# Deferred gate statistics, GpSimd additions in the last chunk, and an unpadded V, in an adaLN + attention + gMLP kernel

## The chip, the core and the metric

The kernel runs on one core of a Trainium2 chip. The metric is the device time of one execution in microseconds (us); lower is better. Three runs of the kernel before the change took 1346.54, 1346.97 and 1347.03 us; their median is 1346.97 us.

## What is computed

One conditioned transformer block on a sequence of 2048 rows of width 512, cut from the reference to what matters here:

```
sa, ca, ga, sb, cb, gb = split(silu(c) @ w_mod, 6)
h = layernorm(x) * (1 + ca) + sa
q = h @ wq                                   # 32 heads of 128; 8 cached K/V heads of 2048 rows
o = softmax(q @ k.T / sqrt(128)) @ v
x = x + ga * (o @ wo)
h = layernorm(x) * (1 + cb) + sb             # "LN2"
z = gelu(h @ w_in)                           # 2048 x 1792
z1, z2 = z[:, :896], layernorm(z[:, 896:])   # z2 is the gate
g = w_sp @ z2 + b_sp[:, None]                # mixes the 2048 rows
y = x + gb * ((z1 * g) @ w_out)
```

Tensors are bfloat16 in memory; sums are kept in float32.

## The kernel before

The 2048 rows are 16 tiles of 128 rows, four tiles to a chunk of 512. Engines are called by their names or by the abbreviations of the profile: TensorE (PE, and PEld for its weight loads), VectorE (DVE), ScalarE (ACT), GpSimd (POOL) and SyncE (SP, which issues most transfers). Each engine works its instructions off in the order in which the program emits them, and that order is written out by hand: `at(it, slot, fn)` hangs a function on a slot of an iteration, and one loop runs through the iterations and their eight slots.

**Attention.** Iteration `it` below NU = 128 is one K/V head and one row tile. In each of its eight slots it multiplies K by q for four query heads (`qk`, L879), exponentiates on ScalarE (L886) and multiplies the previous iteration's probabilities by V (`pv`, L901). V rows have 128 values and a column of ones behind them, so that the matmul also yields the sum of the probabilities; a row thus has 129 columns that are used. The rows lie DV = 136 elements apart in the tile `v1` (L711, printed as `v`), and the two heads of one PSUM bank `o_ps` lie as far apart (L898). L712 fills the columns from 128 on with ones, and L713 loads the values. L912 and L913 normalise by the sum; SP transposes the result (L921).

**Output projection and LN2.** Three iterations later `wo_proj` multiplies by wo (L933); VectorE adds the result to the tile's accumulator (L946), and for the last K/V head also multiplies by ga (L951), adds x (L952) and takes the tile's statistics for LN2 (L690, L691). `ln2` then hangs three steps on later slots: POOL computes the reciprocal deviation (L671, L675), VectorE normalises (L679, `xn`) and SP transposes (L970), VectorE scales and shifts into hT (L977).

**The MLP's first half, inside iterations 128 to 133.** There `zrun(3)` takes three functions at a time off the list `zq`. It holds first the gate tiles 0 to 11 (`z2_tile`): eight matmuls into a two-bank PSUM buffer s_ps (L1064), a Gelu on ScalarE into `z2` (L1074, printed as `z`), then on VectorE two statistics instructions and their aggregation (L1081, L1082). After each fourth tile follows `z2_norm` of that chunk: POOL computes four reciprocal deviations (L671, L675), and VectorE normalises four tiles in place (L679). Then come the seven z1 tiles of the sequence's first half (`z1_tile`, L1100, Gelu L1108). s_ps has two buffers in all.

After iteration 130 the pool `late` is closed (it holds `pT`, `v1`, `wo_g`, `onorm`, `oT` and the accumulators `xacc`), and the pool `mlp` is opened in its place, with z1T, the weights w_out and b_sp (loaded by POOL's queue, L1160 and L1161), and later two blocks of w_sp. What is written into `mlp` must wait until the last use of `late` is through. After the loop SP is given 32 transposing loads of w_sp (L1012), the rest of `zq` is run, then gate tiles 12 to 15, their normalisation, and the other half of z1.

**The MLP's second half.** For each chunk t of output rows, `spatial` accumulates 16 matmuls over the normalised gate tiles (L1205), and VectorE adds b_sp (L1214, `gb`) and multiplies by z1 (L1215, `yT`). `o2_mm` multiplies by w_out (L1220), and `finish_tile` multiplies by gb (L1235, `tmp`) and adds x (L1236, `yout`), both on VectorE, and stores (L1237). `tmp` and `yout` have two buffers each. The last chunk is done in two parts, of 384 and of 128 columns; in the second part the first three output tiles are finished between the spatial matmuls of f = 1 to 3, and the fourth, in two halves, at the very end.

Of the kernel before, what the change touches and what calls it, by code (L numbers as in the profile page):

```python
# [11 lines left out]
FP32 = mybir.dt.float32  # L12
ACT = mybir.ActivationFunctionType
ALU = mybir.AluOpType
AX = mybir.AxisListType
P = 128
# [4 lines left out]
def _f_chunk(f: int) -> int:  # L21
    for cand in range(512, 0, -1):
        if f % cand == 0:
            return cand
    return 1
# [550 lines left out]
def kernel(  # L576
# [19 lines left out]
    nc = tc.nc  # L596
    _, S, D = A_x.shape
    _, HKV, SK, DH = A_k_cache.shape
# [11 lines left out]
    CT = 512 // P  # L610
    FC = _f_chunk(FH)
    NFHC = FH // FC
    NSLOT = NKT // 2
    DV = DH + 8
    inv_sqrt_dh = 1.0 / math.sqrt(DH)

    NB = HKV * NCH
# [1 line left out]
    out_dram = out[0].rearrange("(t p) d -> p t d", p=P)  # L619
# [18 lines left out]
    stat = fast.enter_context(tc.tile_pool(name="stat", bufs=2))  # L638
# [6 lines left out]
    x_sb = res.tile([P, NT, D], BF16, name="x_sb")  # L645
# [6 lines left out]
    mvz = res.tile([P, NT, nc.vector.BN_AGGR_DIM], FP32, name="mvz")  # L652
# [9 lines left out]
    def bank(name):  # L662
        return psum.tile([P, 512], FP32, name=name)

    def bank2():
        return psum.tile([P, 1024], FP32, name="s_ps")

    def rstd_of(mv, n, tag):

        ve = stat.tile([P, CT], FP32, name=f"ve_{tag}")  # L670
        nc.gpsimd.tensor_scalar(  # L671
            out=ve[:, :n], in0=mv[:, :, 1], scalar1=LN_EPS, scalar2=None, op0=ALU.add
        )
        rstd = stat.tile([P, CT], FP32, name=f"rstd_{tag}")
        nc.gpsimd.tensor_tensor(out=rstd[:, :n], in0=ve[:, :n], in1=mhalf[:, :n], op=ALU.pow)  # L675
        return rstd

    def normalise(dst, src, mv, rstd):
        nc.vector.tensor_scalar(  # L679
            out=dst,  # L680
            in0=src,
            scalar1=mv,
            scalar2=rstd,
            op0=ALU.subtract,
            op1=ALU.mult,
        )
# [23 lines left out]
    def load_v(g, rows, engine):  # L710
        v1 = late.tile([P, NKT, DV], BF16, name="v1")  # L711
        nc.gpsimd.memset(v1[:, :, DH:DV], 1.0)  # L712
        engine.dma_start(out=v1[:, :, 0:DH], in_=rows[:, g])  # L713
        groups[g]["v1"] = v1
# [109 lines left out]
    for hf in range(2):  # L824
        nc.scalar.copy(
            out=kT0[:, hf * SK // 2 : (hf + 1) * SK // 2],
            in_=k_ps[:, hf * SK // 2 : (hf + 1) * SK // 2],
# [36 lines left out]
    NU = HKV * NT  # L864
# [3 lines left out]
    def at(it, slot, fn):  # L868
        later.setdefault((it, slot), []).append(fn)
# [23 lines left out]
    def pv(u, i):  # L893
# [3 lines left out]
        if i % (2 * per) == 0:  # L897
            o_pss[u] = bank("o_ps")[:, 0 : 2 * DV].rearrange("p (h d) -> p h d", h=2)  # L898
        o_ps = o_pss[u]
# [156 lines left out]
    zs = {}  # L1056

    def z2_tile(j):
        ps = {}

        def mm(hf, dt):
            if hf == 0 and dt == 0:
                ps[0] = bank2()
            nc.tensor.matmul(  # L1064
                ps[0][:, hf * 512 : hf * 512 + FC],
                lhsT=h2Ts[j // CT][:, dt, (j % CT) * P : (j % CT + 1) * P],
                rhs=win_sb[:, dt, FH + hf * FC : FH + (hf + 1) * FC],
                start=(dt == 0),
                stop=(dt == NDT - 1),
            )  # L1070
            if hf < NFHC - 1 or dt < NDT - 1:
                return
            z2 = zs["z2"]
            nc.scalar.activation(  # L1074
                out=z2[:, j, :].rearrange("p (h c) -> p h c", h=NFHC),
                in_=ps[0][:].rearrange("p (h c) -> p h c", h=2)[:, 0:NFHC, 0:FC],
                func=ACT.Gelu_apprx_tanh,
            )
            stz = stat.tile([P, NFHC, nc.vector.BN_STATS_DIM], FP32, name="stz")
            for h in range(NFHC):  # L1080
                nc.vector.bn_stats(out=stz[:, h, :], in_=z2[:, j, h * FC : (h + 1) * FC])  # L1081
            nc.vector.bn_aggr(out=mvz[:, j, :], in_=stz[:])  # L1082

        return [lambda hf=hf, dt=dt: mm(hf, dt) for hf in range(NFHC) for dt in range(NDT)]

    def z2_norm(ch):
        rstd = rstd_of(mvz[:, ch * CT : (ch + 1) * CT, :], CT, "lnz")
        for j in range(ch * CT, (ch + 1) * CT):
            z2 = zs["z2"]
            normalise(  # L1090
                z2[:, j, :], z2[:, j, :], mvz[:, j, 0:1], rstd[:, j % CT : j % CT + 1]
            )

    def z1_tile(f, ch2):
        ps = {}

        def mm(k, dt):
            if k == 0 and dt == 0:
                ps[0] = bank2()
            nc.tensor.matmul(  # L1100
                ps[0][:, k * 512 : (k + 1) * 512],
                lhsT=win_sb[:, dt, f * P : (f + 1) * P],
                rhs=h2Ts[2 * ch2 + k][:, dt, :],
                start=(dt == 0),
                stop=(dt == NDT - 1),
            )
            if k == 1 and dt == NDT - 1:
                nc.scalar.activation(  # L1108
                    out=zs["z1T"][:, f, ch2 * 1024 : (ch2 + 1) * 1024],
                    in_=ps[0][:],  # L1110
                    func=ACT.Gelu_apprx_tanh,
                )

        return [lambda k=k, dt=dt: mm(k, dt) for k in range(2) for dt in range(NDT)]

    zq = []
    for j in range(3 * CT):
        zq += z2_tile(j)
        if j % CT == CT - 1:
            zq[-1] = [zq[-1], lambda ch=j // CT: z2_norm(ch)]  # L1120
    for f in range(NFT):
        zq += z1_tile(f, 0)
    zq = [z if isinstance(z, list) else [z] for z in zq]

    def zrun(n):
        for _ in range(min(n, len(zq))):
            for fn in zq.pop(0):
                fn()

    for it in range(NU + 6):  # L1130
        if it < NU:
# [31 lines left out]
    for t in range(1, 3):  # L1163
        wsp[t] = mlp.tile([P, NT, 512], BF16, name=f"wsp{t}")
        for st in range(NT):
            load_wsp(wsp[t], t, st)
    zrun(len(zq))
    for j in range(3 * CT, NT):
        for fn in z2_tile(j):
            fn()  # L1170
    z2_norm(3)
    for f in range(NFT):
        for fn in z1_tile(f, 1):
# [5 lines left out]
        out=ok1[:], in0=rall[:], scalar1=1.0 / SAFE, scalar2=None, op0=ALU.is_ge  # L1179
# [8 lines left out]
        out=bad[:], in0=okm[:], scalar1=-1.0, scalar2=1.0, op0=ALU.mult, op1=ALU.add  # L1188
# [10 lines left out]
    z2, z1T = zs["z2"], zs["z1T"]  # L1199

    def spatial(t, yT, f, c0, n):

        g_ps = bank("misc")
        for st in range(NT):
            nc.tensor.matmul(  # L1205
                g_ps[:, :n],
                lhsT=z2[:, st, f * P : (f + 1) * P],
                rhs=wsp[t][:, st, c0 : c0 + n],
                start=(st == 0),
                stop=(st == NT - 1),  # L1210
            )
        cols = slice(t * 512 + c0, t * 512 + c0 + n)
        gb = mlp.tile([P, 512], BF16, name="gb", bufs=2)
        nc.vector.tensor_tensor(out=gb[:, :n], in0=g_ps[:, :n], in1=bsp_bc[:, cols], op=ALU.add)  # L1214
        nc.vector.tensor_tensor(  # L1215
            out=yT[:, f, c0 : c0 + n], in0=gb[:, :n], in1=z1T[:, f, cols], op=ALU.mult
        )

    def o2_mm(dst, yT, jj, f):
        nc.tensor.matmul(  # L1220
            dst,
            lhsT=yT[:, f, jj * P : (jj + 1) * P],
            rhs=wout_sb[:, f, :],
            start=(f == 0),
            stop=(f == NFT - 1),
        )

    def finish_tile(t, jj, src, parts=1):
        j = t * CT + jj
        tmp = mlp.tile([P, D], FP32, name="tmp", bufs=2)  # L1230
        yout = mlp.tile([P, D], BF16, name="yout", bufs=2)
        w = D // parts
        for k in range(parts):
            s = slice(k * w, (k + 1) * w)
            nc.vector.tensor_tensor(out=tmp[:, s], in0=src[:, s], in1=gb_rows[:, s], op=ALU.mult)  # L1235
            nc.vector.tensor_tensor(out=yout[:, s], in0=tmp[:, s], in1=x_sb[:, j, s], op=ALU.add)  # L1236
            (nc.sync if k == 0 else nc.scalar).dma_start(out=out_dram[:, j, s], in_=yout[:, s])  # L1237

    yTs = {}

# [6 lines left out]
    last = NCH - 1  # L1247
# [16 lines left out]
    o2_last = [acc[jj // 2][:, (jj % 2) * 512 : (jj % 2 + 1) * 512] for jj in range(CT)]  # L1264
# [8 lines left out]
    for f in range(NFT):  # L1273
        spatial(last, yT, f, n_a, P)
        if f == 0:
            for jj in range(CT - 1):
                o2_mm(o2_last[jj], yT, jj, NFT - 1)
        else:
            o2_mm(o2_last[CT - 1], yT, CT - 1, f - 1)
        if 1 <= f < CT:  # L1280
            finish_tile(last, f - 1, o2_last[f - 1])
    o2_mm(o2_last[CT - 1], yT, CT - 1, NFT - 1)
    finish_tile(last, CT - 1, o2_last[CT - 1], parts=2)
    fast.close()

    redo = nc.values_load(flag[0:1, 0:1], min_val=0, max_val=P)
# [35 lines left out]
```

## Time and profile before

| | before |
|---|---|
| median of three runs | 1346.97 us |
| the profiled execution | 1347.03 us |
| its span | 1345.2 us (1.83 us lie around it) |
| TensorE busy (PE) | 1303.1 us, 97% |
| weight loads (PEld) | 860.4 us, 64% |
| ScalarE busy (ACT) | 1079.2 us, 80% |
| VectorE busy (DVE) | 476.3 us, 35% |
| GpSimd busy (POOL) | 46.4 us, 3% |
| the chain that ended last | PE 92%, DVE 3%, SP's queue 2%, issue 1%, DMA 1% |

The chain is followed back from the last instruction to what released each step. By lines it is L879 35%, L901 34%, L843 7%, L933 6%, L1205 6%. The page also cuts the span into 40 slices of 33.6 us and gives each engine's busy share in a slice as one digit of tenths; `PEclk` is the clock that TensorE was granted, in tenths of full speed. A line of a timeline has the start, the duration, the engine, the line of the program, the operation, what it writes and reads, its shape and count, and in square brackets the idle time ahead of it and what ended it. A matmul's printed duration contains its pipeline's latency, so the rate of several is read from their starts. A row of a group has the count, then busy time and mean duration of one in ns, then the idle time before.

### The profile page before, as it was taken

The numbers are of one execution on the slowest core, as the hardware profiler recorded it, in microseconds if no ns is written. First come the engines' busy times: TensorE is split into PE (matmuls) and PEld (weight loads), VectorE is DVE, ScalarE is ACT, GpSimd is POOL, SyncE is SP. The second block draws the span as 40 slices with busy tenths as digits, with TensorE's granted clock in tenths as the row PEclk, the third lists the DMA queues.
The fourth block names the chain that finished last, engine by engine and source line by source line (L and its number), as shares of the span: only waits on it lengthen the run. The fifth ranks groups of instructions, "written<-read, shape, count | busy, mean of one in ns | idle before, by whom it ended". The sixth has DMA issues, their size and how long they took to land.

```text
span 1345.2 us, 27642 instructions
## 1 busy us (share of the span) xinstructions
PE 1303.1 (97%) x12137; PEld 860.4 (64%) x12345; DVE 476.3 (35%) x1171; ACT 1079.2 (80%) x1059; POOL 46.4 (3%) x88
## 2 busy tenths in 40 slices
PE   6999999999999999999999999999999999979997
PEld 4666666666666666666666666666666666534444
DVE  5442222222222222222222222222222666873344
ACT  4789999999999999999999999999999999540000
POOL 1010000000000000000000000000000000110000
PEclk9999999999999999999999999999999999989999
DMA  8120021102211120012010410121111111143200
GB/s 274 29 64 17 13 63 37 21 17 35 62 20 21 32 68 17 17 37 68 17 20 13 84 21 17 21 64 32 21 20 17 29 29 33 25 110 83 67 20 26
DMA packets 141184, 56.53 MB, mean 42 GB/s; under 512 B 131105, under 2 KB 136353, under 8 KB 141057
## 3 DMA queue, kind: packets, MB, share of 16 engines
q1 hardware_dynamic: 137504, 42.17, 15.0%
q0 software_dynamic: 3408, 12.45, 3.5%
q8 instruction: 98, 1.61, 0.5%
q14 instruction: 30, 0.24, 0.1%
q10 hardware_dynamic: 144, 0.07, 0.0%
HBM read 21.63 MB, written 2.10 MB: 18 GB/s over the span
## 4 chain that ended last, share of the span: by engine, by line
PE 92%; DVE 3%; SPq 2%; issue 1%; DMA 1%; POOL 0%; ACT 0%; ACTq 0%; POOLq 0%; DVEq 0%
PE s_ps L879 35%; PE o_ps L901 34%; PE misc L843 7%; PE misc L933 6%; PE misc L1205 6%; PE s_ps L1100 2%; SPq L1012 1%; PE o_ps L1220 1%; PE s_ps L1064 1%; DMA wq_g<-in_A_wq_dram 1%; DVE stz L1081 1%; DVE hT L803 0%; PE s_ps L1220 0%; PE misc L796 0%; DVE bnst L690 0%
## 5 line engine op out<-in xcount | busy, mean ns | idle before, releaser
L886 ACT ACTIVATE pT<-s_ps 128x1024 bf16<-128x1024 f32 x1024 | 1045.6, 1024 | 92.2 <-PE s_ps L879 16.5
L901 PEld LDWEIGHTS <-pT 128*128 128x128 bf16 x8192 | 548.5, 98 | 241.2
L901 PE MATMUL o_ps<-v,pT 128*128 128x129 bf16 x8192 | 631.4, 220 | 0.0
L879 PE MATMUL s_ps<-qT,kT 128*128 128x512 bf16 x2048 | 609.9, 379 | 10.8 <-DVE qT L852 0.8
L912 DVE RECIPROCAL rall<-o_ps 128x2 f32<-128x2 f32 x256 | 43.6, 170 | 750.9 <-PE o_ps L901 750.7
L879 PEld LDWEIGHTS <-kT 128*128 128x128 bf16 x2048 | 199.8, 98 | 120.1 <-issue 1.3
L843 PE MATMUL misc<-hT,wq_g 128*128 128x512 bf16 (+2 forms) x462 | 169.1, 376 | 0.8 <-DMA wq_g<-in_A_wq_dram 0.8
L933 PE MATMUL misc<-wo_g,oT 128*128 128x512 bf16 x386 | 146.3, 379 | 0.0
L913 DVE TENSOR_TENSOR onorm<-o_ps,rall 128x256 bf16<-128x256 f32 x256 | 108.7, 425 | 8.8
L1205 PE MATMUL misc<-wsp,z 128*128 128x512 bf16 (+2 forms) x555 | 100.5, 336 | 1.8 <-DVE gb L1214 1.3
L852 DVE CAST qT<-misc 128x512 bf16<-128x512 f32 (+1 forms) x129 | 87.2, 676 | 1.0 <-PE misc L843 1.0
L1205 PEld LDWEIGHTS <-z 128*128 128x128 bf16 x560 | 50.7, 98 | 50.3 <-issue 1.8
L946 DVE TENSOR_TENSOR xacc<-misc,xacc 128x512 f32<-128x512 f32 x112 | 76.2, 680 | 0.0
L843 PEld LDWEIGHTS <-wq_g 128*128 128x128 bf16 x528 | 51.8, 99 | 3.6 <-DMA wq_g<-in_A_wq_dram 1.0
L933 PEld LDWEIGHTS <-oT 128*128 128x128 bf16 x512 | 50.1, 98 | 0.7
L1214 DVE TENSOR_TENSOR gb<-misc,bsp_bc 128x512 bf16<-128x512 f32 (+2 forms) x35 | 20.4, 584 | 60.9 <-PE misc L1205 60.9
L1100 PE MATMUL s_ps<-hT,win_sb 128*128 128x512 bf16 x109 | 26.5, 401 | 7.3 <-ACT z1T L1108 7.1
L1108 ACT ACTIVATE z1T<-s_ps 128x1024 bf16<-128x1024 f32 x14 | 14.2, 1024 | 19.5 <-PE s_ps L1100 10.9
L1064 PE MATMUL s_ps<-win_sb,hT 128*128 128x448 bf16 x128 | 27.0, 352 | 0.1
L1074 ACT ACTIVATE z<-s_ps 128x896 bf16<-128x896 f32 x16 | 14.7, 917 | 14.9 <-PE s_ps L1064 14.9
L712 POOL MEMSET v<- 128x128 bf16 x8 | 1.6, 205 | 705.9 <-issue 606.9
L1100 PEld LDWEIGHTS <-win_sb 128*128 128x128 bf16 x112 | 11.5, 102 | 21.9 <-issue 10.1
(68 smaller groups left out, 288.6 us busy)
## 6 DMA issues: line engine op xcount, KB each, us to landing
v<-in_A_v_cache_dram POOLq DMA_DIRECT2D x7, 512.0 KB, 6.6
wo_g<-in_A_wo_dram POOLq DMA_DIRECT2D x7, 512.0 KB, 4.8
wq_g<-in_A_wq_dram POOLq DMA_DIRECT2D x7, 512.0 KB, 6.0
wsp<-in_w_mod_dram SPq DMA_DIRECT2D x1, 2048.0 KB, 9.2
oT<-onorm SPq DMA_TRANSPOSE x128, 2.4
out_dram<-yout SPq DMA_DIRECT2D x15, 128.0 KB, 1.7
win_sb<-in_B_w_in_dram SPq DMA_DIRECT2D x1, 1792.0 KB, 13.6
wmod_a<-in_w_mod_dram SPq DMA_DIRECT2D x1, 1024.0 KB, 5.4
```

The lines of the kernel that those rows point to most:

```text
L843: nc.tensor.matmul(ps[0][:, o0 : o0 + n], lhsT=wqs[g][:, dt, hh * DH : (hh + 1) * DH], rhs=hTs[ch][:, dt, c0 : c0 + n], start=(dt == 0), s ...
L852: nc.vector.tensor_copy(out=qTs[b][:, hs[0] : hs[-1] + 1, c0 : c0 + n], in_=ps[0][:, 0 : len(hs) * n].rearrange("p (h q) -> p h q", q=n),)
L879: nc.tensor.matmul(s_ps[:, h * 512 : (h + 1) * 512].rearrange("p (r q) -> p r q", r=REP), lhsT=groups[g]["kT"][:, kt * P : (kt + 1) * P], ...
L886: nc.scalar.activation(out=pTs[u][:, 2 * i : 2 * i + 2, :], in_=s_ps[:].rearrange("p (k q) -> p k q", k=2), func=ACT.Exp, scale=inv_sqrt_dh,)
L901: nc.tensor.matmul(o_ps[:, hh % 2, 0 : DH + 1], lhsT=pTs[u][:, kt, hh * P : (hh + 1) * P], rhs=groups[g]["v1"][:, kt, 0 : DH + 1], start=( ...
L912: nc.vector.reciprocal(out=rall[:, c0 : c0 + 2], in_=o_ps[:, :, DH])
L913: nc.vector.tensor_tensor(out=onorms[u][:, hh - 1 : hh + 1, :], in0=o_ps[:, :, 0:DH], in1=rall[:, c0 : c0 + 2].unsqueeze(2).to_broadcast([ ...
L933: nc.tensor.matmul(X_ps[:], lhsT=oTs[u][:, hh, :], rhs=groups[g]["wo"][:, hh, :], start=(hh == 0), stop=(hh == REP - 1),)
L946: nc.vector.tensor_tensor(out=xaccs[j][:], in0=X_ps[:], in1=xaccs[j][:], op=ALU.add)
L1064: nc.tensor.matmul(ps[0][:, hf * 512 : hf * 512 + FC], lhsT=h2Ts[j // CT][:, dt, (j % CT) * P : (j % CT + 1) * P], rhs=win_sb[:, dt, FH + ...
L1100: nc.tensor.matmul(ps[0][:, k * 512 : (k + 1) * 512], lhsT=win_sb[:, dt, f * P : (f + 1) * P], rhs=h2Ts[2 * ch2 + k][:, dt, :], start=(dt ...
L1205: nc.tensor.matmul(g_ps[:, :n], lhsT=z2[:, st, f * P : (f + 1) * P], rhs=wsp[t][:, st, c0 : c0 + n], start=(st == 0), stop=(st == NT - 1),)
```

## The change

The change has three parts.

1. `z2_tile` ends with its Gelu. The statistics are a function of their own, `z2_stats`, hung on slots: tile 0 on iteration 129, tiles 1 and 2 on iteration 130, tiles 3 to 5 on 131, tile 6 on 132 and tiles 7 to 11 on 133, where `z2_norm` of the three chunks follows them. For tiles 12 to 15 the order stays.
2. `finish_tile` takes the engines of its addition. For the last chunk's first three tiles POOL adds; of the fourth tile POOL adds the first half of the columns and VectorE the other, behind both halves' multiplications.
3. DV is 130, not 136: rows of V and the two heads in `o_ps` lie six elements closer, and the memset of ones is as much narrower.

```
-    DV = DH + 8
+    DV = DH + 2
...
-            stz = stat.tile([P, NFHC, nc.vector.BN_STATS_DIM], FP32, name="stz")
-            for h in range(NFHC):
-                nc.vector.bn_stats(out=stz[:, h, :], in_=z2[:, j, h * FC : (h + 1) * FC])
-            nc.vector.bn_aggr(out=mvz[:, j, :], in_=stz[:])
...
+    def z2_stats(j):
+        z2 = zs["z2"]
+        stz = stat.tile([P, NFHC, nc.vector.BN_STATS_DIM], FP32, name="stz")
+        for h in range(NFHC):
+            nc.vector.bn_stats(out=stz[:, h, :], in_=z2[:, j, h * FC : (h + 1) * FC])
+        nc.vector.bn_aggr(out=mvz[:, j, :], in_=stz[:])
...
-        if j % CT == CT - 1:
-            zq[-1] = [zq[-1], lambda ch=j // CT: z2_norm(ch)]
...
+    at(NU + 1, 7, lambda: z2_stats(0))
+    at(NU + 2, 3, lambda: z2_stats(1))
+    at(NU + 2, 4, lambda: z2_stats(2))
+    for j in range(3, 6):
+        at(NU + 3, j, lambda j=j: z2_stats(j))
+    at(NU + 4, 2, lambda: z2_stats(6))
+    for j in range(7, 12):
+        at(NU + 5, j - 7, lambda j=j: z2_stats(j))
+    for ch in range(3):
+        at(NU + 5, 5 + ch, lambda ch=ch: z2_norm(ch))
...
     for j in range(3 * CT, NT):
         for fn in z2_tile(j):
             fn()
+        z2_stats(j)
...
-    def finish_tile(t, jj, src, parts=1):
+    def finish_tile(t, jj, src, adders=(nc.vector,)):
...
-        w = D // parts
-        for k in range(parts):
-            s = slice(k * w, (k + 1) * w)
+        w = D // len(adders)
+        cols = [slice(k * w, (k + 1) * w) for k in range(len(adders))]
+        for s in cols:
             nc.vector.tensor_tensor(out=tmp[:, s], in0=src[:, s], in1=gb_rows[:, s], op=ALU.mult)
-            nc.vector.tensor_tensor(out=yout[:, s], in0=tmp[:, s], in1=x_sb[:, j, s], op=ALU.add)
-            (nc.sync if k == 0 else nc.scalar).dma_start(out=out_dram[:, j, s], in_=yout[:, s])
+        for s, eng in zip(cols, adders):
+            eng.tensor_tensor(out=yout[:, s], in0=tmp[:, s], in1=x_sb[:, j, s], op=ALU.add)
+        for k, s in enumerate(cols):
+            (nc.sync, nc.scalar)[k].dma_start(out=out_dram[:, j, s], in_=yout[:, s])
...
-            finish_tile(last, f - 1, o2_last[f - 1])
+            finish_tile(last, f - 1, o2_last[f - 1], (nc.gpsimd,))
...
-    finish_tile(last, CT - 1, o2_last[CT - 1], parts=2)
+    finish_tile(last, CT - 1, o2_last[CT - 1], (nc.gpsimd, nc.vector))
```

In the changed kernel the spatial matmul is line 1217, the z1 matmul 1103, the statistics 1086 and 1087, and the lines of `finish_tile` 1247 to 1251; lines up to 1074 keep their numbers.

More of the change, by code (lines that the diff above doesn't have):

```diff
@@ L1118 @@
         zq += z2_tile(j)
-        if j % CT == CT - 1:
-            zq[-1] = [zq[-1], lambda ch=j // CT: z2_norm(ch)]
     for f in range(NFT):
         zq += z1_tile(f, 0)
-    zq = [z if isinstance(z, list) else [z] for z in zq]
     def zrun(n):
         for _ in range(min(n, len(zq))):
-            for fn in zq.pop(0):
-                fn()
+            zq.pop(0)()
+    at(NU + 1, 7, lambda: z2_stats(0))
[8 more added lines that the diff above has]
+        at(NU + 5, 5 + ch, lambda ch=ch: z2_norm(ch))
     for it in range(NU + 6):
```

## The prediction

> **What bounds the kernel now.** I read the rows of slices first, to see where TensorE is not busy.
>
> ```profile
> PE   6999999999999999999999999999999999979997
> DVE  5442222222222222222222222222222666873344
> PEclk9999999999999999999999999999999999989999
> ```
>
> TensorE is the bound everywhere but in slice 1, slice 36 (1177 to 1211 us) and slice 40. In slice 36 VectorE has its highest digit, 8, and the granted clock its only 8. The busy times by stretch put a size on it (columns: stretch, its length, then busy time and count of PE, PEld, DVE, ACT, POOL, then granted clock, DMA share, GB/s):
>
> ```profile
> 1149.00:1177.70 28.70, 28.54 (x195) 16.31 (x197) 25.14 (x63) 13.47 (x15) 3.66 (x8) 1.00 0.11 23
> 1177.70:1184.84 7.14, 0.00 (x0) 0.00 (x0) 5.48 (x12) 1.07 (x2) 1.95 (x3) 0.81 0.03 5
> 1184.84:1195.49 10.65, 10.59 (x39) 4.40 (x40) 8.45 (x25) 4.96 (x5) 3.06 (x6) 0.81 0.74 197
> ```
>
> TensorE stands still for 7.14 us, then works at a reduced clock. The waits of 1125 to 1195 us say on whom it stands:
>
> ```profile
> ACT z1T L1108 <- DVE x_sb L952: 8.6, 1, 8.6
> PE s_ps L1100 <- ACT z1T L1108: 7.1, 1, 7.1
> ```
>
> The first Gelu of z1 writes z1T, which lies in the memory of the pool `late`; it must wait for that pool's last reader, L952 of LN2's tile 15 on VectorE. TensorE fills two s_ps buffers (f = 0, 1) and the third z1 tile waits for that Gelu. The timeline shows why L952 is late:
>
> ```profile
> 1168.76 0.38 PE L933 MATMUL misc<-wo_g,oT 128*128 128x512 bf16 x1
> ...
> 1173.12 1.12 DVE L1081 BATCH_NORM_STATS2 stz<-z 128x6 f32<-128x448 bf16 x2
> ...
> 1176.83 1.15 DVE L1081 BATCH_NORM_STATS2 stz<-z 128x6 f32<-128x448 bf16 x2
> ...
> 1179.70 1.78 DVE L679 TENSOR_SCALAR z<-z,mvz,rstd_lnz 128x896 bf16<-128x896 bf16 x4 [1.49 <-POOL rstd_lnz L675]
> 1181.39 0.69 DVE L946 TENSOR_TENSOR xacc<-misc,xacc 128x512 f32<-128x512 f32 x1
> ...
> 1182.84 0.69 DVE L952 TENSOR_TENSOR x_sb<-xacc,x_sb 128x512 bf16<-128x512 f32 x1
> ...
> 1183.77 1.94 ACT L1108 ACTIVATE z1T<-s_ps 128x1024 bf16<-128x1024 f32 x2 [8.57 <-DVE x_sb L952]
> ```
>
> Tile 15's last matmul ends at 1169.14, but VectorE takes its result (L946) at 1181.39: 12 us of gate statistics and normalising stand in its queue.
>
> **Part 1, deferred statistics.** No instruction is added or removed; their order on VectorE and POOL changes, and TensorE's, ScalarE's and SP's orders stay. The after-kernel's VectorE order in this stage, with the spacings of the rows (L946 to the end of L952 2.14 us, to the end of the tile's statistics 3.0; two L1081 and L1082 1.28; xn 0.35; four hT 0.9; one normalise 0.445):
>
> - Tile 13: L946 at 1158.7 (onorm done, L933 done at 1158.33), statistics done 1161.7, POOL 1.1, xn and hT(12) until 1164.2; stats(0) until 1165.5.
> - Tile 14: 1165.5 to 1168.5; stats(1), stats(2) until 1171.0; xn, hT(13) until 1172.3.
> - Tile 15: L946 at 1172.3, L952 ends at **1174.4**, not 1183.53.
>
> TensorE finishes f = 0 at about 1175.9 (eight at 0.2155 from 1174.08), its Gelu ends at 1177.0, and f = 2 would start at 1177.5. L952 may end as late as 1176.2 without delaying it: a margin of 1.8 us. So the 7.14 us go whole. The 40 matmuls between 1184.84 and 1195.49 took 10.65 us; at the 0.2155 each of the undisturbed ones they take 8.62, so **2.03 us** more go with the idle, since the clock in the stretch before it is 1.00. Sum **9.17**.
>
> What is late next? LN2 of tile 15: stats(3), (4), then xn at 1177.9. POOL, whose queue holds the two weight loads (1.05 and 0.59, also released by L952) ahead of tile 15's rstd, delivers it at 1177.7. SP's transpose lands in 2.4 (median row), with stats(5), hT(14), stats(6) meanwhile; hT(15) is done at 1182.6. TensorE needs it at 1195.49 - 9.17 = 1186.3. SP's 32 loads of wsp queue behind that transpose and start some 9 us earlier, as their users do. Then stats(7) to (11) until 1189.0, twelve normalisations until 1194.3 (POOL's third rstd reuses the first one's buffer, free at 1190.8, ready at 1192.2, needed at 1192.6), stats(12) to (15) until 1199.5, POOL 1.5, four normalisations until 1202.8. The spatial matmuls start at 1213.63 - 9.17 = 1204.5 and read tile 12 twelve matmuls later, at 1207.0; it is ready at 1201.5. If this cover of 5.5 us were gone, each us beyond would cost a us. Even before's own finish (the four between 1205.58 and 1207.36) would not stall it: tile 12 was ready at 1206.1. The 1.3 us wait near 1261 stays: the stores wait behind wsp loads that the spatial matmuls themselves release.
>
> **Part 2, the last chunk's additions.** The end of the timeline:
>
> ```profile
> 1331.05 0.68 DVE L1235 TENSOR_TENSOR tmp<-s_ps,gb_rows 128x512 f32<-128x512 f32 x1
> ...
> 1331.77 0.69 DVE L1236 TENSOR_TENSOR yout<-tmp,x_sb 128x512 bf16<-128x512 f32 x1
> ...
> 1332.38 0.28 DVE L1214 TENSOR_TENSOR gb<-misc,bsp_bc 128x128 bf16<-128x128 f32 x1
> ...
> 1335.36 0.38 PE L1220 MATMUL s_ps<-wout_sb,yT 128*128 128x512 bf16 x1 [1.10 <-DVE tmp L1235]
> ...
> 1338.48 0.39 PE L1220 MATMUL s_ps<-wout_sb,yT 128*128 128x512 bf16 x1 [0.43 <-DVE yT L1215]
> ...
> 1340.62 0.38 ACTq L1237 DMA_DIRECT2D out_dram<-yout  x1
> ```
>
> Three multiply-add pairs of 1.4 us delay the small gb and yT operations on VectorE, and TensorE waits for yT. Without the three additions (0.69 each) VectorE keeps up: from 1329.49 TensorE runs six times 16 matmuls and one L1220 at 0.91 + 0.215, ends the last group at 1336.2, gb and yT take 0.55, and the last L1220 starts at 1336.8, not 1338.48: 1.65 us. Behind it VectorE now runs two multiplications (0.34 apart) and one addition in place of two of each: its store is issued 1.25 after the first multiplication, not 1.71: 0.45. POOL's half addition must fit into that. No POOL addition is in the trace. From below its 512 columns take VectorE's 0.69; from above I take twice the nearest POOL row: the affine select of L199 (masks.py), 293 ns for 128 columns of one input. A one-column memset on POOL takes 103, so a column costs (293 - 103) / 128 = 1.5 ns, 512 columns 0.87 us, and two inputs at most twice that, 1.7. I take 1.2, between them. Even at 1.7 the three additions fit: POOL starts them at 1331.9, 1333.6, 1335.5 (after the first store landed), and the half one is done at 1338.6, 2.0 before 1340.62. In range, part 2 gives 1.3 to 2.1; I take **1.9**.
>
> The Trainium skill, "GPSIMD Engine Reference", section "Performance versus the Vector engine", speaks against this part: it has POOL about twice as slow as VectorE for two-input additions, 4497 ns for 2048 columns. An estimate from that page is 1.1 us for 512, and part 2 by it is the same 1.9. No run here shows it yet.
>
> **Part 3, the pitch of v.** Rows of 272 bytes become 260, the memset 128x32; no count changes. v is loaded some 100 us ahead of use and lands in 6.6, so a slower load is hidden. What could cost is the 8192 matmuls that stream v:
>
> ```profile
> L901 PE MATMUL o_ps<-v,pT 128*128 128x129 bf16 x8192 | 631.4, 220 | 0.0
> L1205 PE MATMUL misc<-wsp,z 128*128 128x128 bf16 x112 | 7.4, 219 | 0.2
> ```
>
> Eight of the first take 0.45 (1134.14 to 1134.60, 56.5 ns each), sixteen of the second, whose rows start at multiples of 256 bytes, 0.90 (56 ns). So v as padded is read no slower than plain rows, and dropping the pad can hardly gain: zero from below. No row has a moving operand at 4-byte starts; from above I allow a column's time each, 56.5 / 129 = 0.44 ns, **3.6 us** in all. I take 0, the row it lies nearest to.
>
> The Trainium skill, "SBUF — State Buffer", section "Door 1: The DMA port swizzle", gives SBUF 16-byte lines with a penalty for each new line, which speaks for the old pitch of 17 whole lines. But 258 bytes touch 17 lines from any 4-byte start, so by this rule too the sum stays. No run shows it.
>
> **Sum.** The profiled execution took 1347.03 (span 1345.2 and 1.83 around it; the median shown is 1346.97, the same). 1347.03 - 9.17 - 1.9 = **1336.0**.
>
> **Rivals.**
> - *The stall shrinks but stays* (9 in 100): L952 ends past 1176.2, or POOL's adds hold VectorE. For: VectorE is 88% busy there. Against: the 1.8 us margin. With 1.5 to 6 us of the 11 left: 1337.5 to 1342.
> - *Unaligned v costs a column* (11): 1336.0 + 3.6 = 1339.6.
> - *The stall only moves* (5): the last normalisations become what TensorE waits for, more than 8.5 us past 1207.0: 1344.4 to 1349.7. Against: the cover of 5.5.
> - *Slower* (5): v's starts stall L901, 34% of the chain. From 11.05 / 8192 = 1.35 ns a matmul the gain is lost; at four columns, 1.75 ns, the time is 1336.0 + 14.4 = 1350.4. Against: the 17 lines; for: nothing in the trace excludes it.
>
> **Numbers.** The forecast, 1334.5 to 1337.5, has 70. The range 1334.0 to 1340.5 takes in both bounds of POOL and the column of v. About 0.2% (2.7 us) is what a measurement of this kernel can tell from no change: faster 0.90, same 0.05, slower 0.05.
>
> **What would show it.** Right: no idle of TensorE near 1177, clock 1.00 there, L952 of tile 15 at about 1174, spatial start near 1204.5, last L1220 some 10.8 earlier, eight L901 still 0.45 apart. Wrong: L901's spacing above 0.46 by 3 or more, a wait of L1217 for normalised z, or POOL's additions over 2 us.

## The result: slower by 6.6 us, and the profile after

The changed kernel takes 1353.64 us (median of four runs, 1353.29 to 1353.69) against 1347.00 us for the kernel before on the same chip: a ratio of 1.0045, interval 1.0028 to 1.0063. The forecast of 1336.0 us is missed by 17.6 us and the range by 13. The profiled execution took 1353.61 us, its span 1351.7.

The rows of slices of the kernel after:

```profile
PE   6999999999999999999999999999999999999997
DVE  5442222222222222222222222222222466794344
PEclk9999999999999999999999999999999999999999
```

The dip of TensorE in slice 36 is gone and so is the clock's 8 (mean granted clock 0.999, before 0.996). VectorE has a 9 there now, and TensorE doesn't wait for it. TensorE is busy all the way, and the kernel is slower all the same. So the time must lie in instructions that take longer. Cutting both traces at the same instructions shows which (start times of the instructions named, in us):

| stretch | before | after | difference |
|---|---|---|---|
| start of span to first L901 | 28.1 | 28.4 | +0.3 |
| first L901 to last L901 | 1129.80 | 1144.48 | **+14.68** |
| last L901 to first spatial matmul | 55.74 | 46.41 | **-9.33** |
| first spatial matmul to first of 128 columns | 114.31 | 114.56 | +0.25 |
| from there to the last store's issue | 12.68 | 12.90 | +0.22 |
| from there to the end | 4.6 | 5.0 | +0.4 |

The sum is +6.5, the difference of the spans. Attention pays 14.7 us, the transition gives back 9.3, and the tail gains nothing. Attention goes with part 3, the transition with part 1 and the tail with part 2. The +0.3 at the start is no more than kernels differ there that leave it alone (28.0 to 28.4 us over all runs below).

**Attention (part 3).** Groups of the page after (count, then busy us, mean ns of one, then idle before):

```profile
L901 PE MATMUL o_ps<-v,pT 128*128 128x129 bf16 x8192 | 646.3, 220 | 0.0
L1103 PE MATMUL s_ps<-hT,win_sb 128*128 128x512 bf16 x109 | 24.3, 379 | 0.2
```

The mean duration of L901 is 220 ns as before: it holds the latency and tells nothing. The busy time rose from 631.4 to 646.3. The spacing shows it directly, here eight L901 and their successor on TensorE, in the timeline before and after:

```profile
699.83 0.62 PE L901 MATMUL o_ps<-v,pT 128*128 128x129 bf16 x8
700.28 0.38 PE L933 MATMUL misc<-wo_g,oT 128*128 128x512 bf16 x1
```

```profile
700.06 0.63 PE L901 MATMUL o_ps<-v,pT 128*128 128x129 bf16 x8
700.53 0.38 PE L933 MATMUL misc<-wo_g,oT 128*128 128x512 bf16 x1
```

Eight matmuls now take 0.47 us to the next start, not 0.45. A change of 0.02 us is easily passed over, but there are 1024 such groups: some 15 to 20 us.

**Transition (part 1).** The waits of TensorE between 1140 and 1222 us are none; ScalarE's is

```profile
ACT z1T L1111 <- DVE stz L1086: 0.9, 1, 0.9
```

in place of 8.6. The timeline after, where all times stand 15.0 later than the forecast's (0.3 + 14.68):

```profile
1188.37 0.69 DVE L952 TENSOR_TENSOR x_sb<-xacc,x_sb 128x512 bf16<-128x512 f32 x1
...
1189.05 12.25 PE L1103 MATMUL s_ps<-hT,win_sb 128*128 128x512 bf16 x54
...
1191.10 1.02 ACT L1111 ACTIVATE z1T<-s_ps 128x1024 bf16<-128x1024 f32 x1 [0.94 <-DVE stz L1086]
...
1206.42 1.58 POOL L675 TENSOR_TENSOR rstd_lnz<-ve_lnz,mhalf 128x4 f32<-128x4 f32 x1 [1.33 <-DVE z L679]
...
1216.38 1.78 DVE L679 TENSOR_SCALAR z<-z,mvz,rstd_lnz 128x896 bf16<-128x896 bf16 x4 [1.48 <-POOL rstd_lnz L675]
...
1219.27 2.97 PE L1217 MATMUL misc<-wsp,z 128*128 128x512 bf16 x12
```

L952 of tile 15 ends at 1189.06, ahead of the first Gelu into z1T, so that Gelu starts at 1191.10, some 0.1 us after its own eight matmuls are through (reckoned back from the next Gelu by the 1.73 us between the later ones). The row names a statistics instruction as the last to release it; TensorE doesn't feel it. The 56 matmuls of z1 run without a gap, at full clock by the stretch (columns as before):

```profile
1189.00:1201.13 12.13, 12.03 (x56) 5.48 (x56) 10.83 (x31) 7.06 (x7) 5.11 (x8) 1.00 0.64 174
```

The last four normalisations end at 1218.16; their tiles are read by the spatial matmuls from twelve matmuls behind 1219.27, and none waits.

**Tail (part 2).** The timeline after, of the last chunk's second part:

```profile
1336.80 0.23 DVE L1227 TENSOR_TENSOR yT<-gb,z1T 128x128 bf16<-128x128 bf16 x1
...
1337.58 0.29 DVE L1226 TENSOR_TENSOR gb<-misc,bsp_bc 128x128 bf16<-128x128 f32 x1
1337.70 1.16 POOL L1249 TENSOR_TENSOR yout<-tmp,x_sb 128x512 bf16<-128x512 f32 x1 [121.36 <-DVE tmp L1247]
1337.90 1.04 DVE L1227 TENSOR_TENSOR yT<-gb,z1T 128x128 bf16<-128x128 bf16 x1
1338.86 0.68 DVE L1247 TENSOR_TENSOR tmp<-s_ps,gb_rows 128x512 f32<-128x512 f32 x1
...
1339.00 0.39 PE L1232 MATMUL s_ps<-wout_sb,yT 128*128 128x512 bf16 x1 [0.35 <-DVE yT L1227]
...
1341.51 0.38 PE L1232 MATMUL s_ps<-wout_sb,yT 128*128 128x512 bf16 x1 [1.23 <-DVE tmp L1247]
...
1345.76 0.67 POOL L1249 TENSOR_TENSOR yout<-tmp,x_sb 128x256 bf16<-128x256 f32 x1 [3.06 <-DVE tmp L1247]
1346.05 0.66 DVE L1249 TENSOR_TENSOR yout<-tmp,x_sb 128x256 bf16<-128x256 f32 x1
```

POOL's addition takes 1.16 us, as forecast. But the same yT that took 0.23 us takes 1.04 when it starts beside it, and ends 0.08 after POOL does (1338.86 and 1338.94). The next two take 1.08. What VectorE was relieved of (0.69 an addition) it loses in waiting (0.81 to 0.85). TensorE's wait for `tmp` is 1.23 us, 1.10 before.

### The profile page after: what moved, and what is told of

Read it like the earlier page. It is cut to its first block, busy times and chain, and to the rows that moved or that the text cites. A ratio compares the mean times of both kernels' runs of the same rounds, so it can differ in the third digit from the quotient of the medians.

```text
span 1351.7 us, 27649 instructions
## 1 busy us (share of the span) xinstructions
PE 1316.1 (97%) x12137; PEld 873.2 (65%) x12345; DVE 476.5 (35%) x1167; ACT 1079.7 (80%) x1059; POOL 50.6 (4%) x92
## 4 chain that ended last, share of the span: by engine, by line
PE 94%; DVE 2%; SPq 2%; issue 1%; DMA 1%; POOL 0%; DVEq 0%; POOLq 0%
PE o_ps L901 35%; PE s_ps L879 35%; PE misc L843 7%; PE misc L933 6%; PE misc L1217 6%; PE s_ps L1064 2%; PE s_ps L1103 2%; SPq L1012 1%; PE o_ps L1232 1%; DMA wq_g<-in_A_wq_dram 1%; PE misc L796 0%; DVE hT L803 0%; PE s_ps L1232 0%; DVE xn L679 0%; DVE yT L1227 0%
## 5 line engine op out<-in xcount | busy, mean ns | idle before, releaser
L886 ACT ACTIVATE pT<-s_ps 128x1024 bf16<-128x1024 f32 x1024 | 1046.0, 1024 | 106.5 <-PE s_ps L879 30.4
L901 PEld LDWEIGHTS <-pT 128*128 128x128 bf16 x8192 | 559.6, 98 | 241.7
L901 PE MATMUL o_ps<-v,pT 128*128 128x129 bf16 x8192 | 646.3, 220 | 0.0
L879 PEld LDWEIGHTS <-kT 128*128 128x128 bf16 x2048 | 196.7, 97 | 121.2 <-issue 1.5
L1074 ACT ACTIVATE z<-s_ps 128x896 bf16<-128x896 f32 x16 | 14.7, 917 | 15.0 <-PE s_ps L1064 15.0
L1111 ACT ACTIVATE z1T<-s_ps 128x1024 bf16<-128x1024 f32 x14 | 14.3, 1024 | 10.1 <-PE s_ps L1103 9.1
L690 DVE BATCH_NORM_STATS2 bnst<-x_sb 128x6 f32<-128x512 bf16 x32 | 21.8, 680 | 0.5
```

The source lines that it names most:

```text
L879: nc.tensor.matmul(s_ps[:, h * 512 : (h + 1) * 512].rearrange("p (r q) -> p r q", r=REP), lhsT=groups[g]["kT"][:, kt * P : (kt + 1) * P], ...
L886: nc.scalar.activation(out=pTs[u][:, 2 * i : 2 * i + 2, :], in_=s_ps[:].rearrange("p (k q) -> p k q", k=2), func=ACT.Exp, scale=inv_sqrt_dh,)
L901: nc.tensor.matmul(o_ps[:, hh % 2, 0 : DH + 1], lhsT=pTs[u][:, kt, hh * P : (hh + 1) * P], rhs=groups[g]["v1"][:, kt, 0 : DH + 1], start=( ...
```

## Experiments

### Which part costs: the change with the old pitch

`after_pad` is the kernel after with the one line undone.

```
-    DV = DH + 2
+    DV = DH + 8
```

> The changed kernel with the pitch of 136 columns back in V and o_ps. All three theories on V: the loss of the attention stage goes, so the time is that of before less what parts 1 and 2 bring, 9.1 us and nothing by the traces: 1338 to 1339. If the deferred statistics had a part in the slower attention, more than 1341.

Measured: 1338.79 us, ratio to before 0.9938 (0.9922 to 0.9955). First to last L901 is 1129.80 us, as before; the transition is 46.41 and the tail 12.90, as after. So the 14.7 us come with DV, and the other two parts together are worth 8.9 us, not 11.

### What about DV costs: three single changes to the kernel before

DV sets three things: the start of V's rows within 16 bytes (theory A), the distance of the heads in `o_ps` (theory B), and the distance of V's rows (theory C). Three kernels take one each. Each ratio is to runs of the kernel before on the same chip (medians 1347.47 to 1348.06 us).

`ops_pitch` changes the distance in `o_ps` alone:

```
-            o_pss[u] = bank("o_ps")[:, 0 : 2 * DV].rearrange("p (h d) -> p h d", h=2)
+            o_pss[u] = bank("o_ps")[:, 0 : 2 * (DH + 2)].rearrange("p (h d) -> p h d", h=2)
```

> The kernel before, with only the pitch of the two heads in o_ps taken from 136 to 130 columns. Theory A and theory C: 1347, no change. Theory B: the whole loss of the attention stage is here, about 15 us, 1362.

Measured: 1347.81 us, 1.000 (0.9991 to 1.0010). The output's place costs nothing (theory B falls).

`v_shift4` keeps the pitch of 272 bytes and moves all of V by two elements, so that every row starts 4 bytes past a multiple of 16 (if the tile itself starts at one, which the free rows 0 and 4 of the table below bear out):

```
-        v1 = late.tile([P, NKT, DV], BF16, name="v1")
+        v1 = late.tile([P, NKT * DV + 8], BF16, name="v1")[
+            :, 2 : 2 + NKT * DV
+        ].rearrange("p (t d) -> p t d", d=DV)
```

> The kernel before, with the whole of V moved by 4 bytes: the pitch stays 272 bytes, o_ps stays as it was, but each row now starts 4 bytes past a multiple of 16. Theory A (a moving row that doesn't start at a multiple of 16 bytes costs its matmul about 2.5 ns): all 8192 matmuls pay, 20 us, about 1367 us, and eight of them take 0.474 us in place of 0.453. Theory B (the pitch of the two heads in o_ps, 520 bytes in place of 544): 1347. Theory C (the pitch of 260 bytes itself): 1347.

Measured: 1347.27 us, 0.9998 (0.9988 to 1.0007); attention 1129.80. In its timeline the eight are still 0.45 apart:

```profile
700.10 0.62 PE L903 MATMUL o_ps<-v,pT 128*128 128x129 bf16 x8
700.55 0.38 PE L935 MATMUL misc<-wo_g,oT 128*128 128x512 bf16 x1
```

So an unaligned start costs nothing by itself (theory A falls), which is what the forecast's rival "unaligned v" had priced.

`v_264` has a pitch of 264 bytes, with `o_ps` as before:

```
-    DV = DH + 8
+    DV = DH + 4
```

> The kernel before, with rows of V 264 bytes apart (o_ps as before): every second row starts 8 bytes past a multiple of 16. Theory A: 4096 matmuls pay 2.5 ns, 10 us, about 1357, and within eight matmuls the second, fourth, sixth are long and the others not. Theory B: 1347. Theory C, if only pitches of whole lines are free: as much as at 260, about 1362.

Measured: 1354.62 us, 1.0052 (1.0036 to 1.0069); attention 1137.37, which is +7.57 us: half of what 260 bytes cost, and the time of none of the three forecasts. The two lines of its timeline stand 0.46 apart (0.463 in the median of all groups, 0.453 before, 0.470 after):

```profile
699.98 0.62 PE L901 MATMUL o_ps<-v,pT 128*128 128x129 bf16 x8
700.44 0.38 PE L843 MATMUL misc<-hT,wq_g 128*128 128x512 bf16 x1
```

The step from one start to the next, position by position within the eight, tells more than the sum (ns, my mean over all groups of eight in the trace; position 7 is left out, since other work follows it; its median to that work is 57 before, 60 after, 59 in `v_264`):

```
kernel, row of each eight      0      1      2      3      4      5      6
before, 272 bytes           56.65  56.66  56.67  56.66  56.67  56.67  56.66
after, 260 bytes            56.60  60.89  59.17  59.16  55.84  59.26  59.31
v_264                       56.65  60.83  55.83  59.32  55.83  59.39  55.83
```

At 264 bytes every second matmul pays; at 260 all but rows 0 and 4. A cost of the pitch as such would fall on all of them (theory C falls). Theory A had named the same rows, but `v_shift4` leaves it no cost. What fits both is this (theory D): a row uses 258 bytes, and **a matmul pays when its row's first 16-byte line is the line in which the previous matmul's row ended.** At 260 bytes row 0 ends at byte 257, in the line 256 to 271, and row 1 starts at 260, in the same line. Rows 1, 2, 3, 5, 6 and 7 of each eight share a line so; row 4 starts at 1040 = 65 x 16, a new line. At 264 bytes rows 1, 3, 5 and 7 share; the distance from a row's end to the next start is 6 bytes for all of them there, so the distance alone is not it. At 272 none does, wherever the first row starts. The size of a line follows from the same pattern: with 8-byte lines row 2 at 260 (start 520 = 65 x 8) would be free, with 32-byte lines row 4 (1040, in the line from 1024, where row 3 ends at 1037) would pay. Neither is so.

A rule of the Trainium skill bears on this: "SBUF — State Buffer", section "Door 1: The DMA port swizzle", has SBUF lines of 16 bytes, with full speed for repeated accesses to one line and a penalty for each new one. The unit of 16 bytes agrees with the pattern. The cost goes the other way: here it falls on the row that starts in a line just read, and the row that starts in a new one runs free.

### Sharing a line, or changing the offset: two tests

A rival (E) was left: at 260 and 264 bytes the start's offset within 16 changes from matmul to matmul, and in `v_shift4` it doesn't. `v_276` makes it change (4 bytes more each row) while no two rows share a line.

```
-    DV = DH + 8
+    DV = DH + 10
```

> The kernel before, with V 276 bytes apart: the starts go through 0, 4, 8, 12 within 16 bytes as at 260, but 18 bytes lie between a row's end and the next row's start, so that no line is shared. Theory D: 1347, 0.453 us for eight. Theory E: about 1362, 0.470.

Measured: 1347.27 us, 0.9999 (0.9989 to 1.0008), attention 1129.80:

```profile
700.04 0.62 PE L901 MATMUL o_ps<-v,pT 128*128 128x129 bf16 x8
700.50 0.38 PE L933 MATMUL misc<-wo_g,oT 128*128 128x512 bf16 x1
```

The two starts round to 0.46 apart; the median of all groups is 0.453. In sum the changing offset costs nothing, and E falls as a price. The single steps are not flat, though:

```
kernel, row of each eight      0      1      2      3      4      5      6
v_276                       56.64  58.32  55.86  55.84  56.65  58.33  55.85
```

Rows 1 and 5 take 1.7 ns more, and the rows behind them give it back: four steps come to 226.66 ns, and to 226.64 before. So a step of 58.3 ns by itself does not show a shared line; the sum over the rows has to be read with it.

`v_260_order` has the pitch of 260 bytes (and, like `v_276`, `o_ps` as before) and reads the rows of each eight in the order 0, 2, 4, 6, 1, 3, 5, 7, so that no two that follow each other share a line:

```
-        for kt in range(part * NKT // per, (part + 1) * NKT // per):
+        k0, k1 = part * NKT // per, (part + 1) * NKT // per
+        for kt in [*range(k0, k1, 2), *range(k0 + 1, k1, 2)]:
```

> The kernel before, with V 260 bytes apart as in the change, but each eight matmuls of the second product go through the rows 0, 2, 4, 6, 1, 3, 5, 7, so that no matmul follows the one on the row in front of its own. Theory D (a matmul pays when its row's first 16-byte line is the line in which the matmul before it ended): none pays, 1347, eight matmuls in 0.453 us. Theory E (a matmul pays when its row's start lies otherwise within 16 bytes than that of the matmul before, and not at 0): six of eight still pay, about 1362, 0.470.

Measured: 1349.35 us, 1.0014 (1.0004 to 1.0023); attention 1131.74, that is +1.94 us in place of +14.68.

```profile
700.11 0.62 PE L902 MATMUL o_ps<-v,pT 128*128 128x129 bf16 x8
700.56 0.38 PE L843 MATMUL misc<-hT,wq_g 128*128 128x512 bf16 x1
```

The same bytes read in another order give back 12.7 of the 14.7 us. So nearly all of it is the neighbourhood in time of two rows, not the layout. A remainder of 1.9 us stays, which theory D had not forecast, with steps of 59.17 and 60.01 ns at positions 1 and 5 (rows 2 and 3) and 55.8 at most others. Row 2 shares its first line with row 1 alone, which is read three matmuls later.

`v_260_order2`, with the same pitch, asks whether the remainder comes from reading a line again two matmuls later. Its order is 0, 4, 1, 5, 2, 6, 3, 7, by this line in place of the last one above:

```
+        for kt in [k0 + m // 2 + m % 2 * 4 for m in range(k1 - k0)]:
```

> V 260 bytes apart with o_ps as before, rows in the order 0, 4, 1, 5, 2, 6, 3, 7. Theory D in its strict form (only the matmul directly before counts): 1347, from the first to the last of the second product's matmuls 1129.8 us. If a line read two or more matmuls earlier counts too, or starts off 16 bytes cost a little by themselves, the 1131.7 us of the other order come again.

Measured: 1349.00 us, 1.0008 (0.9998 to 1.0018); attention 1130.96, +1.16. Steps of 58.33 at position 2 and 60.00 at position 6, 55.8 to 56.7 elsewhere. The time lies between the two forecasts. Position 2 (row 1, whose line row 0 read two matmuls earlier) pays, position 4 (row 2, in the same case) doesn't; and `v_276` has the same 58.3 where no line is shared. The remainder of 1.2 to 1.9 us is not settled.

### The line shared without any change of pitch

`cols_136` and `cols_137` keep rows of 272 bytes that start at multiples of 16, and stream more columns: 136 fill the row to its end, and the 137th is the first element of the next row, in the very line with which the next matmul starts. The sums of the extra columns aren't used.

```
-                o_ps[:, hh % 2, 0 : DH + 1],
+                o_ps[:, hh % 2, 0 : 136],
...
-                rhs=groups[g]["v1"][:, kt, 0 : DH + 1],
+                rhs=groups[g]["v1"][:, kt * DV : kt * DV + 136],
```

(with 137 for 136 in the other; `v1` is kept as a flat tile and the heads in `o_ps` lie 144 apart.)

> A control for the next run: the kernel before at its pitch of 272 bytes, with the second product reading 136 columns of each row, to the row's last byte (the seven more are ones, and their sums are not used). Each matmul reads seven columns more, at most 2.9 ns: 1347 + 24 = 1371 at most, about 1364 if a part hides as it seems to at 129. All theories alike: no line is shared.

> The same with 137 columns, so that each row's reading ends in the next row's first element (its sum is not used); every row still starts at a multiple of 16 bytes. Theory D (a line shared with the matmul before costs 2 to 2.5 ns): 3.4 us for the column and 13 to 18 for the seven of eight matmuls that begin in the line where the one before ended: 16 to 21 us above the run of 136 columns. Any theory by the rows' starts: 3.4 us above it.

Measured: 136 columns 1367.59 us, 1.0145 (1.0128 to 1.0162), attention 1149.99; 137 columns 1392.10 us, 1.0326 (1.0309 to 1.0343), attention 1174.50. The first and the second timeline:

```profile
700.57 0.64 PE L903 MATMUL o_ps<-v,pT 128*128 128x136 bf16 x8
701.04 0.38 PE L845 MATMUL misc<-hT,wq_g 128*128 128x512 bf16 x1
```

```profile
700.11 0.66 PE L903 MATMUL o_ps<-v,pT 128*128 128x137 bf16 x8
700.61 0.38 PE L935 MATMUL misc<-wo_g,oT 128*128 128x512 bf16 x1
```

Seven columns cost 20.2 us, 0.35 ns a column and matmul. One more costs 24.5 us, more than the 16 to 21 forecast. A row of 137 columns also touches 18 lines in place of 17, and that could be the price as well. The steps tell the two apart:

```
kernel, row of each eight      0      1      2      3      4      5      6
cols_136                    59.17  59.17  59.17  59.16  59.16  59.17  59.17
cols_137                    59.99  64.16  62.47  62.53  62.65  62.54  62.60
```

Row 0 has the 18th line too, but no matmul of the eight in front of it, and takes 0.82 ns more; the others take 3.3 to 5.0 more. By row 0 the column and its line are worth 6.7 us in all, by the mean price of a column (0.44 ns, 56.66 / 129) 3.6. So 17.8 to 20.9 us fall on the 7168 matmuls that start in a line just read: 2.5 to 2.9 ns each, at aligned starts and the old pitch. This is the direct case for theory D. Its sizes elsewhere: 14.68 us / 6144 = 2.4 ns at 260 bytes, 7.57 / 4096 = 1.85 at 264, where the free rows run at 55.83 and give some back.

### The tail: additions on VectorE again, and inputs in PSUM

`defer_only` is `after_pad` with all additions on VectorE, in the new order.

```
-            finish_tile(last, f - 1, o2_last[f - 1], (nc.gpsimd,))
+            finish_tile(last, f - 1, o2_last[f - 1])
...
-    finish_tile(last, CT - 1, o2_last[CT - 1], (nc.gpsimd, nc.vector))
+    finish_tile(last, CT - 1, o2_last[CT - 1], (nc.vector, nc.vector))
```

> The changed kernel with the padded V and with VectorE doing the additions of the last chunk again: part 1 alone. Theory P (POOL's additions bring as much as they cost): within 0.5 us of the kernel with both, 1338.5 to 1339.3. If POOL's additions bring something, 1340 to 1341; if they cost, 1337 to 1338.

Measured: 1338.20 us, 0.9928 (0.9915 to 0.9942), between the bands for "cost" and for "as much as they cost"; the tail is 12.40 us, against 12.90 with POOL and 12.68 before. So part 1, with the new order of the last tile, is worth 9.3 us, and POOL's additions bring nothing. Behind an addition on VectorE yT is as short as ever:

```profile
1322.93 0.69 DVE L1249 TENSOR_TENSOR yout<-tmp,x_sb 128x512 bf16<-128x512 f32 x1
...
1323.86 0.22 DVE L1227 TENSOR_TENSOR yT<-gb,z1T 128x128 bf16<-128x128 bf16 x1
```

`gb_tmp_psum` is `after_pad`, where VectorE's operations beside POOL's additions have one input in PSUM: for the 128-column tiles `gb` stays in its PSUM bank (so yT reads it there, in float32 and not rounded), and the half tile that VectorE adds keeps its product in PSUM.

```
-        gb = mlp.tile([P, 512], BF16, name="gb", bufs=2)
+        gb = g_ps if n == P else mlp.tile([P, 512], BF16, name="gb", bufs=2)
...
+        mids = [src if len(adders) > 1 and eng is nc.vector else tmp for eng in adders]
+        for s, mid in zip(cols, mids):
+            nc.vector.tensor_tensor(out=mid[:, s], in0=src[:, s], in1=gb_rows[:, s], op=ALU.mult)
+        for s, eng, mid in zip(cols, adders, mids):
+            eng.tensor_tensor(out=yout[:, s], in0=mid[:, s], in1=x_sb[:, j, s], op=ALU.add)
```

> The changed kernel with the padded V; in the last 128 columns VectorE writes gb back into PSUM, and the last tile's VectorE half keeps its product there too, so that no VectorE operation beside POOL's additions has two inputs in SBUF. Theory P1 (a VectorE operation with two SBUF inputs waits until POOL's addition ends): yT takes about 0.3 us in place of 1.04 to 1.08, and the 1.9 us forecast for part 2 come: about 1336.7. Theory P2 (any VectorE operation that starts beside a POOL addition waits): yT stays above 1 us, 1338.8.

Measured: 1337.06 us, 0.9920 (0.9906 to 0.9933), the fastest version here. Its timeline:

```profile
1322.81 0.29 DVE L1226 TENSOR_TENSOR misc<-misc,bsp_bc 128x128 f32<-128x128 f32 x1
1322.97 2.29 POOL L1250 TENSOR_TENSOR yout<-tmp,x_sb 128x512 bf16<-128x512 f32 x2 [121.29 <-DVE tmp L1248]
1323.13 0.29 DVE L1227 TENSOR_TENSOR yT<-misc,z1T 128x128 bf16<-128x128 f32 x1
...
1324.26 0.29 DVE L1227 TENSOR_TENSOR yT<-misc,z1T 128x128 bf16<-128x128 f32 x1
...
1329.30 0.67 POOL L1250 TENSOR_TENSOR yout<-tmp,x_sb 128x256 bf16<-128x256 f32 x1 [2.16 <-DVE tmp L1248]
1329.73 0.42 DVE L1250 TENSOR_TENSOR yout<-s_ps,x_sb 128x256 bf16<-128x256 f32 x1
```

Two POOL additions run from 1322.97 to 1325.26, and the two yT inside them take 0.29 us, not 1.04 and 1.08; VectorE's half addition takes 0.42 beside POOL's, not 0.66. The tail is 11.15 us: 1.75 less than after and 1.53 less than before, where the forecast had wanted 1.9. In yT the input that moved to PSUM also became float32; in the half addition it is float32 in both kernels, and only its place differs. So the delay comes with two inputs in SBUF, as shown by taking one away.

The Trainium skill, "SBUF — State Buffer", section "SBUF: two separate sides", states it: of a GpSimd operation that reads SBUF and a VectorE operation with two SBUF inputs, the one that starts first holds a shared port for its whole instruction, and the other blocks fully. The runs agree, with 0.23 us against 1.04 to 1.08. It spoke against part 2 and was not weighed in the prediction.

## Why the prediction was wrong, step by step

**Part 1 was right, in mechanism and size.** The stretch to the first spatial matmul shrank by 9.33 us (forecast 9.17). Less the shift of 15.0: L952 ends at 1174.1 (1174.4), the last hT(15) is ready at 1183.3 (1182.6), the last normalisation at 1203.2 (1202.8), the spatial matmuls start at 1204.3 (1204.5). Both rivals of this part, the stall that shrinks or moves, are out: TensorE waits for nothing there. Tile 12 was ready at about 1216.8 and read twelve matmuls behind 1219.27, at 1221.9: a cover of 5 us (forecast 5.5), though POOL's power beside the twelve normalisations took 1.58 us in place of 1.04.

**Part 3 failed, and with it the forecast.** The step was "from above I allow a column's time each, 56.5 / 129 = 0.44 ns, **3.6 us** in all. I take 0, the row it lies nearest to". It cost 14.68 us, 1.79 ns a matmul. Two things were wrong in it:

- The bound from above was the price of a column, and no row showed that a stall at a row's start is as short. The row taken as the nearest, L1205, could not show the cost: its rows are 256 bytes at multiples of 256 bytes, so no two share a line. Neither could before's own L901.
- The argument that 258 bytes touch 17 lines from any 4-byte start counts the lines of one row. True, and `v_shift4` confirms that such a start is free; but the pad also kept two rows that follow each other out of one line, and that was not counted.

The rival "Slower" had the place (v's starts stall L901), the point of decision (1.35 ns) and nearly the price (1.75 ns, 14.4 us); its chance of 5 in 100 was too small for a cost that, in its own words, nothing in the trace excluded. The range left it out. Its mechanism is not the measured one, since starts as such are free (`v_shift4`), and no row stood behind its four columns: that the price came close is luck.

**Part 2 failed in the term taken as sure.** POOL's addition was the disputed price and came out right (1.16 us against 1.2). The step that failed is "Without the three additions (0.69 each) VectorE keeps up": VectorE keeps waiting, because yT starts beside each addition and has both inputs in SBUF. Forecast -1.9; measured +0.22 to the last store's issue. Of the stretches around it, the +0.25 ahead and the +0.4 behind are in `defer_only` too (114.62 and 5.2 us), where POOL adds nothing, so they are not POOL's. The rival "POOL's adds hold VectorE" named this, with 1.5 to 6 us of the 11 not gained; without part 3 (`after_pad`, 2.8 us above the forecast) it would have been met. With the delay taken away the tail gains 1.53, so the rest of the forecast for part 2 was a little too high as well.

Three slips in the prediction's figures change nothing: VectorE's highest digit, the 8, stands in slice 35 (slice 36 has a 7); 1338.48 - 1336.8 is 1.68, not 1.65; and the steps of L901 before are 56.66 ns in the mean, not 56.5.

From 1336.0 to 1353.61 the sum is then 14.68 (part 3) + 1.9 + 0.25 + 0.22 + 0.4 (part 2's missing gain and its surroundings) + 0.3 (start) - 0.16 (part 1) = 17.6.

## What to carry to other kernels

Where many short matmuls stream consecutive rows of one tile, pad the rows so that none starts in the 16-byte line in which the one before ended (here 14.7 us at 258 bytes read of each 260), or change the order in which they are read (12.7 of the 14.7 came back); a step of 2 to 3 ns per matmul doesn't show in the mean duration of a group, only in the starts and in a stage's length. Work given to POOL relieves VectorE only where the VectorE operations beside it don't read both inputs from SBUF; leave one in PSUM (yT 0.29 us beside POOL, not 1.04 to 1.08). And when a stall ends on the last reader of a pool that is being reused, look for work in that reader's queue that can come later: this was the part worth 9 us.

## What the runs showed that was not expected

- Matmuls whose moving row starts in the line where the previous one ended are 1.8 to 2.9 ns later; starts at 4 bytes past 16 are free (`v_shift4`), and in sum so are starts that change from row to row (`v_276`).
- Steps of 58.3 to 60.0 ns also fall on rows that share no line with the row just read. At 276 bytes the next steps give them back; at 260 bytes, reordered, 1.2 to 1.9 us remain. No theory here orders them.
- Attention keeps its own beat to 0.01 us: first to last L901 is 1129.80 us in all seven kernels that stream 129 columns at 272 or 276 bytes, so a stage's length settles what medians with a spread of 1 to 3 us leave open.
